# Attention with beacon keys and a gated feed-forward block on one core: out matmuls, first loads and batch 0's value bursts rearranged

## The chip, the cores and the metric

The kernel runs on one core of one Trainium2 chip. The metric is the device time of one execution in microseconds; a kernel's time is the median of several runs.

## The reference

Eight batches of eight heads: softmax attention of 576 queries over 16 beacon keys (seen by all) and 576 causal keys, then a GEGLU block (4,608 tokens, 512 wide, 1,536 inside) on the attention's output.

```python
k_all = np.concatenate([beacon_k, k], axis=2)          # B, H, 16 + 576, 64
v_all = np.concatenate([beacon_v, v], axis=2)
scores = scale * np.matmul(q, k_all.transpose(0, 1, 3, 2))
causal[:, Nb:] = np.triu(np.ones((S, S), dtype=bool), k=1)
scores = np.where(causal, -1000000000.0, scores)
a = softmax(scores)
attn = np.matmul(a, v_all)
x = attn.transpose(0, 2, 1, 3).reshape(B * S, H * D)
g = x @ w_gate
out = (0.5 * g * (1.0 + erf(g * inv_sqrt2)) * (x @ w_val)) @ w_out
```

(`softmax` stands for the four lines that subtract the maximum, exponentiate and divide by the sum.) Inputs and output are float32.

## The kernel before

All matmuls are in bfloat16; the loads [...]are issued on POOL's queue (`dma`, line 111, and line 166). Everything is recorded with `keep`, so each engine runs its instructions in the order in which the program names them: the order of the work is written out by hand.

**Attention.** Heads are taken in pairs (m = 0 to 3), keys in five tiles of 128, 128, 128, 128 and 80 rows. The scores of a pair are computed transposed (keys on the partitions) in four chunks (`CHUNKS`, line 27), causal parts alone. `scores(b, (m, c), ...)` (line 241) takes a tile of the PSUM pool `psum_s`, which has three slots, fills it with matmuls of 64 rows, one per head of the pair, and lets ACT write the exponentials to `exp_ring`. For batch 0 the causal mask is added by small matmuls (`neg`, `eye`); for batches 1 to 7 `masks` (line 287) zeroes the diagonal blocks on POOL, behind whatever POOL has in its queue. `attend` (line 308) multiplies the exponentials with v in 30 matmuls of 65 columns; the 65th column of v is one and gives the sum. Its output takes a slot of `psum_s` as well, or, with where="ot", the single slots of `psum_t` and `psum_o`. `normalize` (line 344) divides on DVE and so frees that slot; `av` is both. The result is turned into `xT_sb` by TensorE and a copy (`turn`, `put`) or, for pairs 0 and 1 of batches 1 to 7, by DMA transposes on SP (`turn_dma`).

**The transposes of q and k.** Batch 0's are made on TensorE by halves (`transpose_both`), batch 1's on TensorE by `transpose_pe` (line 193: 25 small matmuls into a slot of `psum_s`, then copies on DVE), later ones by ten DMA transposes on SP (`transpose_dma`).

**The feed-forward block.** `gate_val(ci, fi)` (line 433) makes one of twelve slices of 128 inner channels for a chunk of 512 tokens: four matmuls with `wg_sb`, four with `wv_sb`, GELU on ACT, the product on DVE into `h_of[ci]`. `out_mms` (line 455) then runs units of one matmul of 512 columns each, 48 for a chunk (four token tiles of twelve slices); with each twelfth, DVE copies the tile out and SP stores it.

**The order.** Batch 0's attention comes first, while the weights load. Then for each b (line 561): for b of 1 to 7 the attention of batch b with the 48 out matmuls of chunk b - 1 dealt between its pieces by `o(n)` (lines 570 to 607), and the twelve gate and value slices of chunk b (line 617). The loads are issued in this order at the start: batch 0's q and k, v of batch 0 in two halves of four heads, gate and value weights in six pairs of two slices, around q and k of batch 1, w_out in three parts, v of batch 1, the first five loads of batch 2; `ahead(2)` issues the remaining loads of batch 2, two at a time, inside batch 1's attention. `warm(100)` (line 523) runs 100 small matmuls on zeroes at the start.

Of the kernel before, what the change touches and what calls it, by code (L numbers as in the profile page):

```python
# [7 lines left out]
P = 128  # L8
B, H, S, NB, D = 8, 8, 576, 16, 64
SK = S + NB  # L10
# [32 lines left out]
FP32 = mybir.dt.float32  # L43
BF16 = mybir.dt.bfloat16
ACT = mybir.ActivationFunctionType
# [6 lines left out]
def kernel(  # L52
# [12 lines left out]
    nc = tc.nc  # L65
    keep = tc.keep_in_program_order
# [7 lines left out]
    psum_s = ctx.enter_context(tc.tile_pool(name="psum_s", bufs=3, space=bass.MemoryType.PSUM))  # L74
    psum_t = ctx.enter_context(tc.tile_pool(name="psum_t", bufs=1, space=bass.MemoryType.PSUM))
    psum_o = ctx.enter_context(tc.tile_pool(name="psum_o", bufs=1, space=bass.MemoryType.PSUM))
# [6 lines left out]
    wg_sb = const.tile([P, K_CHUNKS, D_FF], BF16, name="wg_sb", tag="wg_sb")  # L83
    wv_sb = const.tile([P, K_CHUNKS, D_FF], BF16, name="wv_sb", tag="wv_sb")
# [6 lines left out]
    NRING = 2  # L91
    q_ring, k_ring, v_ring = [], [], []
# [9 lines left out]
    qkT = ring.tile([P, NPAIR, 2, 640], BF16, name="qkT", tag="qkT")  # L102
# [8 lines left out]
    def dma(out_ap, in_ap):  # L111
        keep(nc.gpsimd.dma_start(out=out_ap, in_=in_ap))  # L112
# [19 lines left out]
    def load_kb(b):  # L132
        dma(qk6_of(b)[1], beacon_k[b].rearrange("h t d -> t h d"))

    def key_loads(src, beacon, dst, b, h0=0, h1=H):
        parts = [(dst[0:NB, 0, :, :], beacon[b].rearrange("h t d -> t h d"))] if h0 == 0 else []
        dst, src = dst[:, :, h0:h1, :], src[:, h0:h1, :, :]
        parts.append((dst[NB:P, 0, :, :], src[b, :, 0:112, :].rearrange("h p d -> p h d")))
        for j in range(1, 5):
            n = KROWS[j]  # L140
            r0 = 112 + (j - 1) * P
            parts.append((dst[0:n, j, :, :], src[b, :, r0 : r0 + n, :].rearrange("h p d -> p h d")))
        return [lambda o=o, i=i: dma(o, i) for o, i in parts]
# [12 lines left out]
        for load in qk_loads(b):  # L156
            load()

    def load_v(b, h0=0, h1=H):
        for load in key_loads(v, beacon_v, v_ring[b % NRING][:, :, :, 0:D], b, h0, h1):  # L160
            load()

    def load_gate_val(f0, f1):
        fs = slice(f0 * P, f1 * P)
        for w, dst in ((moe_w_gate, wg_sb), (moe_w_val, wv_sb)):
            keep(nc.gpsimd.dma_start(out=dst[:, :, fs], in_=w[:, fs].rearrange("(kk p) f -> p kk f", p=P)))

    def load_out_w(f0, f1):
        dma(wo_sb[:, f0:f1, :], moe_w_out[f0 * P : f1 * P, :].rearrange("(ii p) m -> p ii m", p=P))
# [1 line left out]
    def mm(out_ap, lhsT, rhs, start, stop, **kw):  # L171
        keep(nc.tensor.matmul(out_ap, lhsT, rhs, start=start, stop=stop, **kw))  # L172

    def act(out_ap, in_ap, func, **kw):
        keep(nc.scalar.activation(out_ap, in_ap, func, **kw))  # L175
# [6 lines left out]
    def tr_part(b, m, w, dst):  # L182
        qk, kb = qk6[b]
        for r in range(6):
            for hi in range(2):
                tr(
                    dst[64 * hi : 64 * hi + 64, r * 96 : (r + 1) * 96],
                    qk[0:96, w, 2 * m + hi, r * D : (r + 1) * D],
                )
        if w:  # L190
            tr(dst[:, S:SK], kb[:, 2 * m : 2 * m + 2, :])

    def transpose_pe(b, m):
        t_ps = psum_s.tile([P, 2, 1024], BF16, name="t_ps", tag="s")
        for w in range(2):
            tr_part(b, m, w, t_ps[:, w, :])
        keep(
            nc.vector.tensor_copy(
                qkT[:, m, :, NB:SK].rearrange("p w (t r) -> p w t r", r=6),
                t_ps[:, 0:2, 0:S].rearrange("p w (r t) -> p w t r", r=6),  # L200
            )
        )
        keep(nc.vector.tensor_copy(qkT[:, m, 1, 0:NB], t_ps[:, 1, S:SK]))

    def transpose_half(b, m, w, by_act=False):
# [19 lines left out]
    def warm(n):  # L225
        w_ps = psum_s.tile([P, 2, 512], FP32, name="w_ps", tag="s")
        for j in range(n):
            mm(w_ps[:, 0, 0:D], idle, idle[:, 0:D], True, True)
# [76 lines left out]

    x_of = {}

    def attend(b, m, where="s", heads=(0, 1)):
        i = b * NPAIR + m
        if heads[0] == 0:  # L310
            attend_tiles(i, where)
        x_ps = x_tiles[i]
        expT, v_sb = exp_ring[:, m, :, :], v_ring[b % NRING]
        for j in range(5):
            for hi in heads:
                for t in range(j + 1):
                    e0 = EXP_OFF[t] + S_LO[j] - S_LO[t]
                    mm(
                        x_ps[hi][:, j * DV : (j + 1) * DV],
                        expT[0 : KROWS[t], hi, e0 : e0 + P],  # L320
                        v_sb[0 : KROWS[t], t, 2 * m + hi, 0:DV],
                        t == 0,
                        t == j,
                        skip_group_check=True,
                    )

    x_tiles = {}

    def attend_tiles(i, where):
        if where == "ot":  # L330
            x_ps = (
                psum_t.tile([P, 512], FP32, name="xt_ps", tag="t"),
                psum_o.tile([P, 512], FP32, name="xo_ps", tag="o"),
            )
            x_of[i] = [(x_ps[hi].rearrange("p (b c) -> p b c", b=1), hi, hi + 1) for hi in range(2)]
        else:
            x = psum_s.tile([P, 2, 512], FP32, name="x_ps", tag="s")
            x_ps = (x[:, 0, :], x[:, 1, :])
            x_of[i] = [(x, 0, 2)]
        x_tiles[i] = x_ps  # L340

    y_of = {}

# [111 lines left out]
    def out_mms(ci, u0, u1):  # L455
        for u in range(u0, u1):
# [15 lines left out]
            out=eye,  # L472
            in_=eye,
# [10 lines left out]
            out=neg,  # L484
            in_=neg,
# [6 lines left out]
    )  # L492
    load_qk6(0, 4, 6)
    load_qk6(0, 6, H)
    load_v(0, 0, 4)
    load_v(0, 4, H)
    for f0 in (0, 2, 4, 6, 8):
        load_gate_val(f0, f0 + 2)
    load_qk6(1, 0, 4)
    load_kb(1)  # L500
    load_gate_val(10, 12)
    load_qk6(1, 4, H)
    for f0 in (0, 4, 8):
        load_out_w(f0, f0 + 4)
# [3 lines left out]
    def ahead(n):  # L508
        for load in loads[:n]:
            load()  # L510
        del loads[:n]
# [3 lines left out]
    def av(b, m, where="s"):  # L515
        attend(b, m, where)
        normalize(b, m)

    def c(*parts):
        scores(0, *parts)  # L520

    keep(nc.scalar.preload_act_table_set(SET_EXP))
    warm(100)
    keep(nc.vector.tensor_copy(qk6[0][1], kb_sb))
    transpose_both(0, 0)
    c((0, 0))
# [9 lines left out]
    transpose_both(0, 3)  # L536
    c((2, 2))
    c((2, 1))
    av(0, 0)
    c((3, 0))  # L540
    c((3, 2))
    av(0, 1, "ot")
    c((2, 3), (3, 3))
    c((3, 1))
    av(0, 2)
    turn(0, 0)
    put(0, 0, by_act=True)
# [13 lines left out]
    for b in range(B):  # L561
        u = [0]

        def o(n):
            out_mms(b - 1, u[0], u[0] + n)
            u[0] += n

        if b:
            keep(nc.scalar.preload_act_table_set(SET_EXP))
            o(4)  # L570
            scores(b, (0, 0))
            scores(b, (0, 2))
            scores(b, (0, 1))
            if b == 1:
                transpose_pe(1, 2)
            o(5)
            ahead(2)
            if b == 1:
                transpose_pe(1, 3)
            o(5)  # L580
            scores(b, (0, 3), (1, 3))
            scores(b, (1, 0))
            scores(b, (1, 2))
            ahead(2)
            o(6)
            av(b, 0)
            turn_dma(b, 0)
            o(2)
            scores(b, (1, 1))
            scores(b, (2, 0))  # L590
            scores(b, (2, 2))
            ahead(2)
            o(6)
            av(b, 1)
            turn_dma(b, 1)
            o(2)
            scores(b, (2, 1))
            scores(b, (2, 3), (3, 3))
            scores(b, (3, 0))
            o(10)  # L600
            scores(b, (3, 1))
            scores(b, (3, 2))
            av(b, 2)
            o(5)
            turn(b, 2)
            put(b, 2)
            o(3)
            av(b, 3)
            keep(nc.scalar.preload_act_table_set(SET_GELU))  # L609
            gv_mms(b, 0, 0, 1, 2)  # L610
            gv_mms(b, 1, 0)
            turn(b, 3)
            put(b, 3)
            gv_mms(b, 1, 1, 2)
            gv_mms(b, 0, 3, last=True)
            gv_mms(b, 1, 3, last=True)
        for fi in range(F_TILES):
            if fi >= 2:
                gate_val(b, fi, fi == F_TILES - 1 and b < B - 1)
            if b == 0 and fi in (8, 9):  # L620
                transpose_pe(1, fi - 8)
            if fi == 0:
                if b and b + 1 < B:
                    load_v(b + 1)
                if b and b + 2 < B:
                    load_qk(b + 2)
                if 2 <= b + 1 < B:
                    transpose_dma(b + 1)
# [39 lines left out]
```

The softmax here doesn't subtract the row's maximum and nothing guards it: scores larger than these inputs give would overflow.

## Time and profile before

| | |
|---|---|
| Median of 8 runs | 379.07 us (378.75 to 380.74) |
| The profiled execution's own time | 379.06 us |
| Its span, first to last instruction | 377.1 us |
| One matmul of 512 columns in a stream, start to start | 0.215 us |
| Batch 2's first scores to batch 3's | 91.8 to 132.0 us |
| Batch 1's value burst 0 | 54.4 to 57.5 us |

The first three rows of the page's costliest groups show what each engine does for the feed-forward block and the scores:

```profile
L175 ACT ACTIVATE ge_sb<-gv_ps 128x512 bf16<-128x512 f32 x101 | 59.4, 597 | 139.4 <-PE gv_ps L172 139.4
L175 ACT ACTIVATE expT<-s_ps 128x960 bf16<-128x960 f32 (+3 forms) x112 | 99.8, 965 | 28.5 <-PE s_ps L172 28.0
L428 DVE TENSOR_TENSOR hT_sb<-gv_ps,ge_sb 128x512 bf16<-128x512 f32 x101 | 69.1, 690 | 106.0 <-ACT ge_sb L175 106.0
```

A row gives line, engine, operation, what is written from what, the shape and the number of instructions; behind the bar the busy time in us and the mean of one in ns, then the idle time of the engine ahead of them and who ended it. Helpers record every matmul on line 172 and every activation on line 175, so tiles tell more than lines. PE is TensorE's matmuls, PEld its weight loads, which overlap them; [...]a stream of 0.38 us matmuls starts one each 0.215 us. A few matmul records are missing in the trace: a run of o_ps x9 can be ten.

### The profile page before, as it was taken

The numbers are of one execution on the slowest core, as the hardware profiler recorded it, in microseconds if no ns is written. First come the engines' busy times: TensorE is split into PE (matmuls) and PEld (weight loads), VectorE is DVE, ScalarE is ACT, GpSimd is POOL, SyncE is SP. The second block draws the span as 40 slices with busy tenths as digits, with TensorE's granted clock in tenths as the row PEclk, the third lists the DMA queues.
The fourth block names the chain that finished last, engine by engine and source line by source line (L and its number), as shares of the span: only waits on it lengthen the run. The fifth ranks groups of instructions, "written<-read, shape, count | busy, mean of one in ns | idle before, by whom it ended". The sixth has DMA issues, their size and how long they took to land.

```text
span 377.1 us, 7611 instructions
## 1 busy us (share of the span) xinstructions
PE 359.1 (95%) x3072; PEld 183.8 (49%) x3122; DVE 151.2 (40%) x253; ACT 186.5 (49%) x240; POOL 166.0 (44%) x293
## 2 busy tenths in 40 slices
PE   7899978999999999999999999999999999999996
PEld 7664434544454445444454445444544454444443
DVE  2553633533344424442353334433444344434332
ACT  3963456435743486338723774357534872322210
POOL 8965578951486246833494158704700330000000
PEclk9999999999999999999999999999999999999999
DMA  7999999999179923996299929991592030000103
GB/s 103 124 176 198 206 168 116 135 136 129 45 126 128 155 43 90 148 154 71 59 145 138 99 72 127 152 111 46 116 135 43 33 86 28 2 0 28 55 32 110
DMA packets 152050, 38.33 MB, mean 102 GB/s; under 512 B 136528, under 2 KB 147536, under 8 KB 152016
## 3 DMA queue, kind: packets, MB, share of 16 engines
q0 software_dynamic: 107184, 19.13, 69.8%
q1 hardware_dynamic: 44832, 18.73, 26.6%
q8 instruction: 24, 0.39, 0.4%
q14 instruction: 10, 0.08, 0.1%
HBM read 38.27 MB, written 9.44 MB: 127 GB/s over the span
## 4 chain that ended last, share of the span: by engine, by line
PE 77%; DMA 9%; DVE 6%; POOL 6%; issue 2%; POOLq 0%
PE gv_ps L172 41%; PE o_ps L172 20%; PE x_ps L172 7%; DVE y_sb L354 5%; PE s_ps L172 5%; DMA wo_sb<-in_moe_w_out_dram 3%; DMA qk<-in_q_dram 3%; DMA wv_sb<-in_moe_w_val_dram 2%; POOL v_sb L112 2%; PE g_ps L172 1%; PE v_ps L172 1%; DVE r_sb L352 1%; PE y_ps L180 1%; POOL qk L112 1%; POOL q_sb L112 1%
## 5 line engine op out<-in xcount | busy, mean ns | idle before, releaser
L175 ACT ACTIVATE ge_sb<-gv_ps 128x512 bf16<-128x512 f32 x101 | 59.4, 597 | 139.4 <-PE gv_ps L172 139.4
L175 ACT ACTIVATE expT<-s_ps 128x960 bf16<-128x960 f32 (+3 forms) x112 | 99.8, 965 | 28.5 <-PE s_ps L172 28.0
L428 DVE TENSOR_TENSOR hT_sb<-gv_ps,ge_sb 128x512 bf16<-128x512 f32 x101 | 69.1, 690 | 106.0 <-ACT ge_sb L175 106.0
L172 PE MATMUL gv_ps<-xT_sb,wv_sb 128*128 128x512 bf16 x402 | 107.7, 379 | 0.1
L172 PE MATMUL gv_ps<-xT_sb,wg_sb 128*128 128x512 bf16 x386 | 105.9, 379 | 0.9
L172 PE MATMUL o_ps<-wo_sb,hT_sb 128*128 128x512 bf16 (+2 forms) x414 | 101.0, 373 | 3.8 <-issue 2.2
L295 POOL TENSOR_SCALAR_AFFINE_SELECT expT<-expT 128x256 bf16<-128x256 bf16 (+2 forms) x140 | 51.6, 386 | 108.4 <-ACT expT L175 107.6
L172 PEld LDWEIGHTS <-wv_sb 128*128 128x128 bf16 x432 | 42.2, 98 | 50.8
L172 PEld LDWEIGHTS <-wg_sb 128*128 128x128 bf16 x432 | 41.2, 98 | 46.9
L172 PEld LDWEIGHTS <-hT_sb 128*128 128x128 bf16 x444 | 38.8, 98 | 43.4 <-issue 6.2
L447 DVE COPY o_sb<-o_ps 128x512 f32<-128x512 f32 (+2 forms) x37 | 25.0, 675 | 44.2 <-PE o_ps L172 44.1
L172 PE MATMUL s_ps<-qkT 64*128 64x512 bf16 (+5 forms) x384 | 33.7, 281 | 5.5 <-DVE y_sb L354 3.2
L112 POOL DMA_DIRECT2D v_sb<-in_v_dram x45 | 36.6, 838 | 3.0 <-DMA wo_sb<-in_moe_w_out_dram 1.7
L172 PEld LDWEIGHTS <-expT 128*128 128x128 bf16 (+1 forms) x960 | 32.9, 97 | 8.8 <-POOL expT L295 1.9
L172 PE MATMUL x_ps<-v_sb,expT 128*128 128x65 bf16 x930 | 34.0, 193 | 1.7 <-POOL expT L295 1.6
L112 POOL DMA_DIRECT2D k_sb<-in_k_dram x30 | 25.2, 842 | 16.9 <-DMA v_sb<-in_v_dram 8.4
L172 PEld LDWEIGHTS <-qkT 64*128 64x128 bf16 x384 | 13.9, 94 | 27.4 <-issue 13.1
L112 POOL DMA_DIRECT2D q_sb<-in_q_dram x30 | 25.3, 887 | 3.5 <-DMA wo_sb<-in_moe_w_out_dram 3.5
L354 DVE TENSOR_TENSOR y_sb<-x_ps,r_sb 128x640 bf16<-128x640 f32 x31 | 25.5, 824 | 1.1
L352 DVE RECIPROCAL r_sb<-x_ps 128x10 f32<-128x10 f32 x31 | 6.8, 221 | 43.7 <-PE x_ps L172 43.7
L387 DVE COPY xT_sb<-y_ps 128x576 bf16<-128x576 bf16 x15 | 6.9, 457 | 10.6 <-PE y_ps L180 10.6
L609 ACT ACT_TABLE_LOAD x7 | 9.0, 1283 | 0.1
(50 smaller groups left out, 127.8 us busy)
## 6 DMA issues: line engine op xcount, KB each, us to landing
out_dram<-o_sb SPq DMA_DIRECT2D x35, 256.0 KB, 2.2
q_sb<-in_q_dram POOLq DMA_DIRECT2D x24, 128.0 KB, 8.9
v_sb<-in_v_dram POOLq DMA_DIRECT2D x21, 128.0 KB, 6.7
k_sb<-in_k_dram POOLq DMA_DIRECT2D x18, 128.0 KB, 9.9
wg_sb<-in_moe_w_gate_dram POOLq DMA_DIRECT2D x6, 256.0 KB, 9.4
wv_sb<-in_moe_w_val_dram POOLq DMA_DIRECT2D x6, 256.0 KB, 9.9
wo_sb<-in_moe_w_out_dram POOLq DMA_DIRECT2D x3, 512.0 KB, 11.9
v_sb<-in_v_dram POOLq DMA_DIRECT2D x7, 112.0 KB, 3.3
```

Of the source, the lines that this page charges most:

```text
L112: keep(nc.gpsimd.dma_start(out=out_ap, in_=in_ap))
L172: keep(nc.tensor.matmul(out_ap, lhsT, rhs, start=start, stop=stop, **kw))
L175: keep(nc.scalar.activation(out_ap, in_ap, func, **kw))
L180: keep(nc.tensor.transpose(out_ap, in_ap, ident[0:n, 0:n]))
L295: nc.gpsimd.affine_select(out=d, in_=d, pattern=[[0, 2], [1, n]], compare_op=ALU.is_ge, fill=0.0, base=NB if t == 0 else 0, channel_multip ...
L352: keep(nc.vector.reciprocal(r, x[:, :, :, D:DV]))
L354: nc.vector.tensor_tensor(out=y_sb[:, :, h0:h1, :].rearrange("p j b d -> p b j d"), in0=x[:, :, :, 0:D], in1=r.to_broadcast([P, h1 - h0, 5 ...
L387: keep(nc.vector.tensor_copy(out_ap, y_ps[:, 0:S]))
L428: nc.vector.tensor_tensor(out=h_of[ci][:, fi, :], in0=gv_of.pop((ci, fi))[1], in1=ge_sb, op=ALU.mult)
L447: keep(nc.vector.tensor_copy(o_sb[:, ti, c0:c1], o_ps))
L609: keep(nc.scalar.preload_act_table_set(SET_GELU))
```

## The change

Six edits go together.

1. In batches 1 to 7 the out matmuls are dealt differently. Before: 4, scores, 10, scores, 6, values 0, 2, scores, 6, values 1, 2, scores, 10, scores, values 2, 5, turn 2, 3, values 3. After: 4, scores, 9, scores, 5, values 0, 4, scores, 5, values 1, 4, scores, 9, scores, values 2, 6, turn 2, 2, values 3.
2. v of batch 0 is loaded in whole key tiles of eight heads (6 DMAs) instead of two halves of four heads (11).
3. Gate and value weights are loaded in slices of 2, 2, 4 and 4 channels' tiles instead of six slices of 2; the last four stand behind the first half of batch 1's q and k, as the last two did.
4. Batch 0's value bursts 0 and 1 stand behind the scores of pairs 2 and 3, burst 0 in `psum_t` and `psum_o` instead of burst 1.
5. Batch 1's transposes stand behind gate slices 6, 7 and 9 of batch 0 (pairs 0, 1, 2) and behind the first scores of batch 1 (pair 3), instead of behind slices 8 and 9 (pairs 0, 1) and inside batch 1 (pairs 2, 3). The copy of q and k becomes two, of which ACT makes the one of q in the gate stage.
6. `warm(100)` becomes `warm(50)`.

`load_v`, `key_loads`, `attend` and `load_gate_val` lose or change the arguments that this needs.

```diff
-    def key_loads(src, beacon, dst, b, h0=0, h1=H):
-        parts = [(dst[0:NB, 0, :, :], beacon[b].rearrange("h t d -> t h d"))] if h0 == 0 else []
-        dst, src = dst[:, :, h0:h1, :], src[:, h0:h1, :, :]
-        parts.append((dst[NB:P, 0, :, :], src[b, :, 0:112, :].rearrange("h p d -> p h d")))
+    def key_loads(src, beacon, dst, b):
+        parts = [
+            (dst[0:NB, 0, :, :], beacon[b].rearrange("h t d -> t h d")),
+            (dst[NB:P, 0, :, :], src[b, :, 0:112, :].rearrange("h p d -> p h d")),
+        ]
...
-    def transpose_pe(b, m):
+    def transpose_pe(b, m, by_act=False):
...
-        keep(
-            nc.vector.tensor_copy(
-                qkT[:, m, :, NB:SK].rearrange("p w (t r) -> p w t r", r=6),
-                t_ps[:, 0:2, 0:S].rearrange("p w (r t) -> p w t r", r=6),
-            )
-        )
+        out_ap = qkT[:, m, :, NB:SK].rearrange("p w (t r) -> p w t r", r=6)
+        in_ap = t_ps[:, 0:2, 0:S].rearrange("p w (r t) -> p w t r", r=6)
+        keep(nc.vector.tensor_copy(out_ap[:, 1], in_ap[:, 1]))
+        if by_act:
+            act(out_ap[:, 0], in_ap[:, 0], ACT.Copy)
+        else:
+            keep(nc.vector.tensor_copy(out_ap[:, 0], in_ap[:, 0]))
...
-    load_v(0, 0, 4)
-    load_v(0, 4, H)
-    for f0 in (0, 2, 4, 6, 8):
-        load_gate_val(f0, f0 + 2)
+    load_v(0)
+    load_gate_val(0, 2)
+    load_gate_val(2, 4)
+    load_gate_val(4, 8)
     load_qk6(1, 0, 4)
     load_kb(1)
-    load_gate_val(10, 12)
+    load_gate_val(8, 12)
...
-    warm(100)
+    warm(50)
...
     c((2, 1))
-    av(0, 0)
     c((3, 0))
     c((3, 2))
-    av(0, 1, "ot")
     c((2, 3), (3, 3))
+    av(0, 0, "ot")
     c((3, 1))
+    av(0, 1)
     av(0, 2)
...
             if b == 1:
-                transpose_pe(1, 2)
-            o(5)
+                transpose_pe(1, 3)
             ahead(2)
-            if b == 1:
-                transpose_pe(1, 3)
-            o(5)
+            o(9)
             scores(b, (0, 3), (1, 3))
             scores(b, (1, 0))
             scores(b, (1, 2))
             ahead(2)
-            o(6)
+            o(5)
             av(b, 0)
             turn_dma(b, 0)
-            o(2)
+            o(4)
...
-            o(6)
+            o(5)
             av(b, 1)
             turn_dma(b, 1)
-            o(2)
+            o(4)
             scores(b, (2, 1))
             scores(b, (2, 3), (3, 3))
             scores(b, (3, 0))
-            o(10)
+            o(9)
             scores(b, (3, 1))
             scores(b, (3, 2))
             av(b, 2)
-            o(5)
+            o(6)
             turn(b, 2)
             put(b, 2)
-            o(3)
+            o(2)
             av(b, 3)
...
-            if b == 0 and fi in (8, 9):
-                transpose_pe(1, fi - 8)
+            if b == 0 and fi in (6, 7, 9):
+                transpose_pe(1, min(fi - 6, 2), by_act=True)
```

## The prediction

> **What bounds the kernel now.** I read the page's busy shares and slices, then the chain of waits, then the timeline around every place where TensorE stands still.
>
> ```profile
> PE 359.1 (95%) x3072; PEld 183.8 (49%) x3122; DVE 151.2 (40%) x253; ACT 186.5 (49%) x240; POOL 166.0 (44%) x293
> DMA  7999999999179923996299929991592030000103
> PE 77%; DMA 9%; DVE 6%; POOL 6%; issue 2%; POOLq 0%
> ```
>
> TensorE sets the end, except where the chain goes through DMA, POOL and DVE: two places, one in the first 57 us and one that comes back in each of batches 1 to 7. The chain in order of time shows the first:
>
> ```profile
> 26.27 10.67 DMA qk<-in_q_dram
> 37.23 13.06 DMA wo_sb<-in_moe_w_out_dram
> 50.57 3.31 POOL q_sb L112 x4
> 53.87 1.38 POOL expT L295 x4
> 55.26 1.29 POOL k_sb L112 x2
> 56.55 0.43 POOL expT L295
> 57.03 0.65 PE x_ps L172 x15
> ```
>
> All loads and all causal masks sit on POOL's one queue. From the ninth DMA on, an issue waits for the landing of the DMA eight issues earlier, so a late transfer holds POOL, the masks of batch 1 behind it, and the value matmuls that read them. The timeline has the result (idle time in brackets):
>
> ```profile
> 50.33 0.38 PE L172 MATMUL o_ps<-wo_sb,hT_sb 128*128 128x512 bf16 x1 [0.79 <-DMA wo_sb<-in_moe_w_out_dram]
> 57.03 0.63 PE L172 MATMUL x_ps<-v_sb,expT 128*128 128x65 bf16 x15 [1.60 <-POOL expT L295]
> ```
>
> The second place, in batch 2 (batches 3 to 7 repeat it within 0.01 us):
>
> ```profile
> 91.81 0.55 PEld L172 LDWEIGHTS <-qkT 64*128 64x128 bf16 x10 [0.42 <-DMA qkT<-k_sb]
> 92.54 1.84 PEld L172 LDWEIGHTS <-hT_sb 128*128 128x128 bf16 x10 [0.17 <-issue]
> ...
> 98.25 0.28 PEld L172 LDWEIGHTS <-qkT 64*128 64x128 bf16 x8 [0.42 <-issue]
> 99.05 0.09 PEld L172 LDWEIGHTS <-qkT 64*128 64x128 bf16 x2 [0.52 <-DVE y_sb L354]
> 99.35 0.98 PEld L172 LDWEIGHTS <-hT_sb 128*128 128x128 bf16 x6 [0.21 <-issue]
> 102.10 0.32 PEld L172 LDWEIGHTS <-qkT 64*128 64x128 bf16 x10 [0.42 <-issue]
> 102.91 0.39 PE L172 MATMUL s_ps<-qkT 64*128 64x512 bf16 x2 [0.25 <-DVE y_sb L354]
> 103.23 1.84 PEld L172 LDWEIGHTS <-hT_sb 128*128 128x128 bf16 x10 [0.23 <-issue]
> 108.27 0.43 PE L180 MATMUL y_ps<-eye,y_sb 112*128 112x112 bf16 x5
> ```
>
> A burst of three score tiles without a wait goes from 91.81 to 92.54, 0.73 us. The burst behind the first value burst takes 98.25 to 99.35, 1.10, the one behind the second 102.10 to 103.23, 1.13: 0.37 and 0.40 us are waits for the normalisation (DVE writes y_sb), which gives back the third PSUM slot of psum_s. From start to start of the single matmuls the waits are 0.37 and 0.41.
>
> **What the Trainium skill says.** *DMA: Bandwidth & Descriptors*, Specifications: transfers below 512 B miss line rate. The trace agrees: at 50 to 54 us the 128 B packets moved 150 GB/s, 512 B ones 197 at 24 to 38, 1 KB ones 206 at 40 to 46. Its Anatomy section puts any semaphore wait of a DMA on the issuing sequencer; that is the POOL chain above. *Trainium Kernel Development and Optimization*, Best Practices: consistent bubbles can mean that PSUM ran out; here 0.37 us in each batch. *TensorE: Matmul & The Clock Gate*, Part 1: the array runs at half clock until some 3.4 us of activity in a free-running window. The trace agrees: the warm matmuls start 53 ns apart until 5.5 us, then 29.
>
> **The change part by part.** Sums are against the profiled execution: span 377.1, time 379.06, 1.96 outside the span; the median of the runs, 379.07, is the same.
>
> *Out matmuls redistributed, batches 1 to 7.* All 48 stay. An out matmul in a stream costs 0.215 us. Behind a value burst stand 4 instead of 2: 0.43 us, so the third score tile comes to its slot when it is free. In batch 2 y_sb ends 1.1 us after the value burst; four out matmuls, the switch (0.1) and two score tiles (0.41) take 1.37, the first wait goes whole. The third tile of the second burst would come at 102.50 + 0.43 = 102.93 against 102.91: just gone. One more ahead of `turn(b,2)`: five end at 108.01, the transposes waited until 108.27; six end at 108.22, 0.21 gained. Sum 0.37 + 0.41 + 0.21 = 0.99 a batch.
> What is late next: two fewer out matmuls ahead of value burst 0 and burst 1 meet the masks 0.43 to 0.58 earlier. ACT and POOL move too: exp of the burst before starts 0.21 earlier, so mask (0,3) is done at 96.38, value burst 0 starts at 96.38 and reads it 12 matmuls (0.4) later. For burst 1 the exp of (1,1) keeps its time (two fewer ahead, two more behind); its mask ends at 100.18, the burst starts at 100.08 and reads it at 100.3; the tail tile 100.45 against 100.8. Value burst 2 needs the slot of (3,0): its exp ends at 105.08, it comes at 105.22. All fit, with 0.1 to 0.4 us in hand; each miss would cost at most that order. The transposes into xT_sb on SP start 0.43 earlier, ending on SP at 107.7, landed by 108.8 (2.3 more for the last one at most); the gate stage reads them at 109.3. Loads and transposes of the next batch start with the stage's end, move with it, and have the unchanged 21 us gate stage as cover: today the last qkT transpose lands 0.2 to 0.35 us before its reader, and the spacing of both stays.
>
> *v of batch 0 in whole tiles.* 11 issues become 6: at 0.73 to 0.88 us each POOL ends them at 12.1 instead of 15.2. The data are the same 128 B packets; packets a microsecond were 1,044 at 12 to 13 but 700 to 770 at 13 to 16, issue-bound, against up to 1,180 elsewhere. At 1,100 the 4,736 packets end near 15.3 instead of 16.8: the weights start 1.5 us sooner.
>
> *Weights in four-chunk slices (first two pairs excepted).* 12 gate and value DMAs become 8, each half as many packets of 1 KB: 512 B packets went at 383 a microsecond, 1 KB at 200, so 1.34 x 2 = 2.67 against 2.56 us, 0.11 x 4 = 0.45 gained. Between 16 and 22 us the trace lost another 1.5 us of DMA rate (130 GB/s instead of 197) for no reason that I can read; whether that stays is unknown: 0 to 1.5, I take 0. Later slices are needed as a whole: the value half of 8 to 11 lands at about 37.4 (40.2 less 2.0, less reordering), its first reader comes near 38; I price it at 0 (up to 0.6), covered by the slack below.
> So w_out and the queries behind it land 2.0 us sooner (1.95), between 0 and 3.5. POOL's masks, 53.87 today, follow at 51.9 and the waiting value matmuls at 55.0.
>
> *Transposes of batch 1 moved* (three into batch 0's gate stage, one left after the first scores; half of the copy on ACT). 0.87 us each on TensorE, the same number. In the gate stage ACT works 0.60 of each 1.73 us, DVE 0.69, so ACT's 0.65 and DVE's 0.76 + 0.15 are hidden. They need qk landed: 32.2 and 40.0 estimated against 33.7 and 40.6. One 0.88 wait for a score slot stays.
>
> *Warm-up 50, and batch 0's values behind the last scores.* The first keys land at 4.43, the queries at 5.28, but the transposes start at 6.19 behind the warm matmuls. With 50 these end at 3.9; the first exp could start 1.3 us earlier, less if the array stays at half clock. The value burst gives no score slot away, so ACT's 0.27 wait goes.
> None of this shows in the end: TensorE would reach the masked tile of batch 1 at 54.58 - 0.95 (w_out wait gone) - 0.43 (two out matmuls later) + 0.4 = 53.6 even with no gain here, and the mask comes at 55.0. Value 0; cover 1.4 us, 2.7 if the 1.3 come. The two out matmuls pushed behind that wait cost 0.43 in batch 1, once.
>
> Sum: 2.0 + (0.99 - 0.43) + 6 x 0.99 = 8.5. Span 368.6, time 370.6.
>
> **The rivals.**
> 1. *Forecast*: both gains, 370.6, and 369 if the lost DMA rate comes back too. Chance 0.65; its own range is 368.4 to 372.
> 2. *The load chain keeps its time.* DMA is 90% busy there whatever POOL does; then only 6.5 goes: 372.6. For it: the rate between 16 and 22 us was low though eight DMAs were queued. Against it: the issue-bound stretch. 0.13.
> 3. *A new wait takes half of each batch's gain* (mask (1,1), exp (3,0), or the qkT landing, each within 0.1 to 0.35): 6 x 0.5 = 3.0 less, 373.6. For it the thin margins, against it that each was worked out as met. 0.14.
> 4. *Slower: the array stays at half clock.* 50 matmuls last 2.7 us instead of 4.3, and the trace shows the full clock only after 4.3. Batch 0's 16 us of attention hold some 3.3 of waits; 12.7 us at half rate would end 9.4 later. Less 3.4 to the mask wait, less the 6.5 of the batches, that still isn't slower; each further microsecond of gate stage costs 0.5, so it decides only if half clock lasts past about 33 us, and then gives 380 and more. Against it: dense matmuls of 4.3 us raised the clock before. 0.05.
> 5. *No effect*, the waits only change place: 379. 0.03.
>
> **How the numbers follow.** The time is that of rival 1. Range 368.4 to 373.7: it takes in cases 1 and 2 and most of 3. A difference below 0.2% (0.8 us) can't be told from none here. Faster: 0.92 (1 to 3), same 0.03 (5), slower 0.05 (4).
>
> **What would show it.** In the changed profile: score bursts behind values 0.73 us long, no DVE y_sb ahead of s_ps; 39.2 us from batch to batch instead of 40.2; wv of slices 0 to 1 landed near 20.6 instead of 22.3; the wait for w_out gone; the mask wait of batch 1 still there, ending near 55.0. Wrong: batches at 39.7 or more with a wait on POOL expT or ACT expT in their place; the end of the mask wait still near 57; matmuls at half rate after 10 us.

## The result, and the profile after

The changed kernel takes 372.62 us (371.10 to 373.61), 6.5 less than the median shown; against the runs of the kernel before that were taken beside it, the ratio is 0.9814, 95% interval 0.9794 to 0.9834. The forecast was 370.6 with a range of 368.4 to 373.7. The profiled execution took 371.72, its span is 369.7, 7.4 less than the 377.1 of before. From the trace, first scores to first scores:

| us | before | changed | forecast of the difference |
|---|---|---|---|
| start to batch 1 | 46.25 | 48.77 | 0, or up to 0.9 with the third transpose |
| batch 1 to 2 | 45.56 | 40.73 | with the row above: -2.6 |
| batch 2 to 7 (five) | 201.12 | 196.90 | -4.95 |
| batch 7 to the end | 84.15 | 83.26 | -0.99 |

Two page lines (the busy shares of the engines, and the chain of work that ended last by engine):

```profile
PE 358.3 (97%) x3022; PEld 183.7 (50%) x3072; DVE 149.5 (40%) x254; ACT 188.3 (51%) x243; POOL 160.3 (43%) x284
...
PE 87%; DMA 6%; ACT 2%; issue 2%; POOL 1%; DVE 1%; POOLq 0%; ACTq 0%
```

TensorE is busy 97% instead of 95%, and holds 87% of the chain instead of 77%; DVE's share of the chain fell from 6% to 1%, POOL's from 6% to 1%. The timeline of the changed kernel shows where DVE went (batch 2, the score bursts behind value bursts 0 and 1):

```profile
96.03 0.79 PE L176 MATMUL s_ps<-qkT 64*128 64x64 bf16 x10
...
96.76 0.76 PEld L176 LDWEIGHTS <-hT_sb 128*128 128x128 bf16 x5 [0.25 <-issue]
...
99.72 0.78 PE L176 MATMUL s_ps<-qkT 64*128 64x64 bf16 x12
...
100.42 1.63 PEld L176 LDWEIGHTS <-hT_sb 128*128 128x128 bf16 x9 [0.24 <-issue]
```

From the first score to the weight load of the next out matmul it takes 0.73 and 0.70 us, where 1.10 and 1.13 were; no y_sb stands in brackets any more. And where POOL went (batch 1):

```profile
46.07 3.31 POOL L112 DMA_DIRECT2D q_sb<-in_q_dram  x4 [1.67 <-DMA wo_sb<-in_moe_w_out_dram]
...
47.81 1.02 PE L176 MATMUL o_ps<-wo_sb,hT_sb 128*128 128x512 bf16 x4
...
48.77 0.79 PE L176 MATMUL s_ps<-qkT 64*128 64x512 bf16 x10
...
50.28 0.70 PE L184 MATMUL t_ps<-eye,qk 96*64 96x96 bf16 x24 [0.71 <-ACT expT L179]
...
50.30 0.37 POOL L300 TENSOR_SCALAR_AFFINE_SELECT expT<-expT 128x224 bf16<-128x224 bf16 x1 [0.93 <-ACT expT L179]
...
54.85 1.08 PE L176 MATMUL x_ps<-v_sb,expT 128*128 128x65 bf16 x30
```

POOL comes off the last landing of w_out at 46.07 instead of 50.57, so its queue is empty at 49.4, and at 50.30 it is POOL that waits for work (for ACT's exponentials), and no value matmul waits for POOL. The value burst at 54.85 runs its 30 matmuls in 1.08 us with nothing ahead of them; before, 15 of them waited until 57.03. But the first scores of batch 1 come 2.5 us later: 0.87 is the third set of transposes, which now stands ahead of them, and 1.62 the later first gate matmul (23.76 instead of 22.14). In batch 4 a wait shows that this profile of the kernel before doesn't have:

```profile
168.11 0.76 PE L176 MATMUL s_ps<-qkT 64*128 64x512 bf16 x8
...
169.15 0.10 PEld L176 LDWEIGHTS <-qkT 64*128 64x128 bf16 x2 [0.53 <-DMA qkT<-k_sb]
169.16 0.21 PE L176 MATMUL s_ps<-qkT 64*128 64x80 bf16 x2 [0.29 <-DMA qkT<-k_sb]
```

### The profile page after: what moved, and what is told of

It is laid out like the page before. It is cut to its first block, busy times and chain, and to the rows that moved or that the text cites. A ratio compares the mean times of both kernels' runs of the same rounds, so it can differ in the third digit from the quotient of the medians.

```text
span 369.7 us, 7504 instructions
## 1 busy us (share of the span) xinstructions
PE 358.3 (97%) x3022; PEld 183.7 (50%) x3072; DVE 149.5 (40%) x254; ACT 188.3 (51%) x243; POOL 160.3 (43%) x284
## 4 chain that ended last, share of the span: by engine, by line
PE 87%; DMA 6%; ACT 2%; issue 2%; POOL 1%; DVE 1%; POOLq 0%; ACTq 0%
PE gv_ps L176 41%; PE o_ps L176 25%; PE s_ps L176 7%; PE x_ps L176 7%; DMA q_sb<-in_q_dram 3%; DMA qkT<-k_sb 2%; PE t_ps L184 2%; ACT expT L179 2%; PE y_ps L184 1%; PE v_ps L176 1%; PE g_ps L176 1%; POOL v_sb L112 1%; DMA qk<-in_k_dram 1%; DVE qkT L219 0%; DVE y_sb L351 0%
## 5 line engine op out<-in xcount | busy, mean ns | idle before, releaser
L176 PE MATMUL gv_ps<-xT_sb,wg_sb 128*128 128x512 bf16 x400 | 107.8, 379 | 0.2
L176 PE MATMUL gv_ps<-xT_sb,wv_sb 128*128 128x512 bf16 x390 | 104.1, 379 | 0.4
L112 POOL DMA_DIRECT2D v_sb<-in_v_dram x40 | 33.6, 863 | 5.9 <-DMA wv_sb<-in_moe_w_val_dram 1.7
L176 PEld LDWEIGHTS <-qkT 64*128 64x128 bf16 x384 | 14.2, 96 | 22.5 <-issue 15.2
L184 PE MATMUL t_ps<-eye,qk 96*64 96x96 bf16 x192 | 7.9, 238 | 1.3 <-ACT expT L179 0.7
```

The costliest lines, as they stand in the source:

```text
L184: keep(nc.tensor.transpose(out_ap, in_ap, ident[0:n, 0:n]))
```

## The experiments

The edits are given against the kernel named in each heading; "changed" is the kernel after, "before" the one before. Medians stand beside runs of the kernel before on the same chip (379.66 for e1 to e4, 380.32 for e5 to e8, 379.97 for e9 and e10), so times of different sessions are best compared by their ratios; where only one time is given, there was one run.

### e1: changed, with the old warm-up

```diff
-    warm(50)
+    warm(100)
```

> The changed kernel with 100 warm matmuls again. Theory 1 (the array stays at half clock until 15.3 us after 50 of them and TensorE, no longer the load chain, sets batch 1's first value burst): full clock near 5.6 us, batch 1's first scores near 47.1 instead of 48.8 us, no wait for POOL in value burst 0, time 371.0 (370.4 to 371.6). Rival (TensorE's start is covered by the mask wait as the prediction had it, and the missing 2 us lie in the batches): 372.6 as the changed kernel, first scores earlier but the value burst ends at the same time.

Measured: 370.7 us (369.96 to 374.05), ratio 0.9774 [0.9737, 0.9810]. By the trace's record of the granted clock, it is full from 5.21 us on instead of 15.31, the first gate matmul starts at 22.55 instead of 23.76, and everything behind it follows by the same 1.21: batch 1's first scores 47.56. The changed kernel's own timeline shows the half rate, and its end, in two sets of transposes of twelve:

```profile
12.41 0.69 PE L184 MATMUL t_ps<-eye,qk 96*64 96x96 bf16 x12
...
15.64 0.45 PE L184 MATMUL t_ps<-eye,qk 96*64 96x96 bf16 x12
```

The half rate ahead of a trace's first clock record shows in such durations alone: the clock column of the windows further down counts that time as full.

Batch 1 to batch 2 takes 40.73 in both, although the last part of w_out lands at 46.92 here and at 45.78 there: TensorE set batch 1's first value burst, no longer the loads.

### e2 and e3: before, with one part each

e2 has edit 1 alone, e3 has edits 2 and 3 alone:

```diff
-            o(6)
+            o(5)
             av(b, 0)
             turn_dma(b, 0)
-            o(2)
+            o(4)
...
-    load_v(0, 0, 4)
-    load_v(0, 4, H)
-    for f0 in (0, 2, 4, 6, 8):
-        load_gate_val(f0, f0 + 2)
+    load_v(0)
+    load_gate_val(0, 2)
+    load_gate_val(2, 4)
+    load_gate_val(4, 8)
...
-    load_gate_val(10, 12)
+    load_gate_val(8, 12)
```

> The kernel before with the out matmuls dealt as in the changed kernel, nothing else. Theory 1 (the waits for the normalisation go): batches 39.3 us apart instead of 40.2, six times 0.92 and 0.5 in batch 1, 373.1 (372.7 to 373.8). Rival (a new wait takes half): 376.

> The kernel before with v of batch 0 in whole tiles and the weights in 2, 2, 4, 4, nothing else. Theory 1 (the load chain is 4.5 us shorter, whatever else changes): last w_out part lands near 45.8, the w_out wait (0.95) and the mask wait (1.77 and 0.19) both go, 376.2. Prediction's own size (2.0 us): w_out near 48.3, mask wait still there, 377.1. Rival (the load chain is shorter in the changed kernel for another reason): 379.

Measured: e2 374.36 (373.72 to 375.93), ratio 0.9860 [0.9830, 0.9890]; e3 377.01 (376.94 to 377.04), 0.9924 [0.9898, 0.9949]. In e2 the batches take 39.30 to 39.48 but one, 40.07, in which TensorE waited 0.69 for a transpose of k; batch 1's mask wait is still there. In e3 they stay at 40.23 but one, 40.67, w_out lands at 45.68, and the w_out wait and the mask wait are gone; batch 1 to 2 takes 42.61 instead of 45.56. The masked value burst of batch 1 in e2, then in e3:

```profile
57.17 0.63 PE L172 MATMUL x_ps<-v_sb,expT 128*128 128x65 bf16 x15 [1.60 <-POOL expT L295]
```

```profile
54.11 1.08 PE L172 MATMUL x_ps<-v_sb,expT 128*128 128x65 bf16 x30
```

So the two gains are separate: 5.3 and 2.65 of the 8.96 that e1 gained in the same session. Each is somewhat smaller than expected, and 1.0 of the 8.96 is in neither. The profiles of e2 and e3 were held up by what the edits don't touch: the clock was full 1.2 to 1.6 us later than in the profile of before (7.20 and 6.75 instead of 5.58), so batch 1 began 0.70 and 0.49 us later, and late transposes of k cost 0.95 and 0.44.

### e4: before, with the short warm-up

```diff
-    warm(100)
+    warm(50)
```

> The kernel before with 50 warm matmuls, nothing else. Theory 1: half clock until about 15 us, batch 0 ends 1.6 us later, but the mask wait of batch 1 (1.77 and 0.19) shrinks by as much, time 379.1 (378.8 to 379.5). Rival (it isn't covered): 380.7. Rival (clock rises in time, as the prediction took it): transposes from 4.6 us, time 379.1, first scores of batch 1 at or before 46.3.

Measured: 380.0 (378.62 to 381.84), ratio 1.0008 [0.9987, 1.0029]. The clock was full at 4.05, half again at 7.47 and full at 14.29, steps of 3.41 us and of twice that. Batch 1's first scores come 0.41 later, batch 1 to 2 takes 0.33 less: the mask wait swallows most of the loss, as the prediction had it for this edit. The same edit costs 1.2 us in the traces once the mask wait is gone (e1 against the changed kernel; 1.9 between the medians, which are of different sessions). This profile also shows that a late transpose of k doesn't come from the new dealing alone. With the old dealing its batch 2 takes 40.66 instead of 40.23:

```profile
92.89 0.21 PE L172 MATMUL s_ps<-qkT 64*128 64x80 bf16 x2 [0.25 <-DMA qkT<-k_sb]
```

### e5 and e6: which part of the loads

Both on e1; e5 puts v of batch 0 back into halves, e6 the weights into slices of two.

```diff
-    load_v(0)
+    load_v(0, 0, 4)
+    load_v(0, 4, H)
...
-    load_gate_val(4, 8)
+    load_gate_val(4, 6)
+    load_gate_val(6, 8)
...
-    load_gate_val(8, 12)
+    load_gate_val(8, 10)
+    load_gate_val(10, 12)
```

> The changed kernel with 100 warm matmuls and v of batch 0 in two halves again (11 issues), weights as changed. Theory 1 (the issue-bound stretch of v costs 1.5 us, the lost DMA rate from 16 to 22 us goes with the smaller number of weight DMAs): last w_out part lands near 47.5 to 48, v packets at 700 a microsecond from 13 to 16 us, full rate after. Rival (the halves of v cause both losses): the rate from 16 to 22 us is low again, w_out lands near 49 to 50.

> The changed kernel with 100 warm matmuls and all weights in slices of 2 again, v whole. Theory 1 (the larger slices give 0.45 us by their packets and the back-to-back issues of small slices cause the lost rate): w_out near 47.5, rate low from 16 to 22 us. Rival (the halves of v cause the loss): rate full, w_out lands near 46.3, 0.45 later than with the large slices.

Measured: e5 374.59, span 372.6, w_out lands at 49.81; e6 370.94, span 368.9, w_out lands at 46.98 against 46.92 in e1. v in whole tiles is nearly all of the gain. The slices' size gains TensorE nothing: batch 1 to 2 takes 40.73 in e6 as in e1. What it does to the loads can't be told. The last landing of w_out lies between 45.68 and 46.92 in the seven profiles with v whole and slices of four, 1.2 us apart, and the first part of w_out lands at 40.58 to 41.23 in them and at 41.40 in e6, so the forecast's 0.45 is neither shown nor excluded. In e5's timeline the old wait is back:

```profile
56.08 1.47 POOL L299 TENSOR_SCALAR_AFFINE_SELECT expT<-expT 128x256 bf16<-128x256 bf16 x4
56.57 0.51 PEld L175 LDWEIGHTS <-expT 128*128 128x128 bf16 x15 [1.72 <-POOL expT L299]
56.57 0.63 PE L175 MATMUL x_ps<-v_sb,expT 128*128 128x65 bf16 x15 [1.60 <-POOL expT L299]
```

Right behind it the granted clock is half from 57.2 to 60.6, so in this execution the wait costs more than its own length: batch 1 to 2 takes 44.44, 3.71 more than in e6.

### e11c and e12c: why the weights ran slowly behind v in halves

Both on e1, and both without the DMA transposes, so that only their first 56 us are to be read. e11c keeps v whole and puts eight small operations on POOL ahead of the first weight slice; e12c makes eleven DMAs of v by key rows instead of by heads.

```diff
     load_v(0)
+    for _ in range(8):
+        keep(nc.gpsimd.affine_select(out=fill, in_=fill, ...))
     load_gate_val(0, 2)
```

```diff
-    load_v(0)
+    for j in range(5):
+        for p0 in (0, 64):
...
+            dma(v0[p0:p1, j, :, :], v[0, :, r0 : r0 + p1 - p0, :].rearrange("h p d -> p h d"))
```

> The kernel of e1 (changed kernel, 100 warm matmuls) with eight small operations on a scratch tile on POOL between the loads of v and the first weight slice. Left out: the DMA transposes; batches 2 to 7 have no new qkT (they score with batch 1's), and pairs 0 and 1 are turned by TensorE and DVE, so that only the first 56 us are to be read, and the span is no measure. v stays in whole key tiles; the first weight issue moves from 12.06 to about 15.6 us, where it stood with v in halves (e5: 15.53). It asks why the weights behind the halves of v also ran slowly (e5: 304 to 347 packets of 512 B a microsecond at 18 to 23 us, against 339 to 385 in e1). Theory A (the late issue alone: the DMA queue has run down when the weights come): packets of 512 B at 300 to 345 a microsecond through 18 to 22 us, the last part of w_out lands near 49.5 (e1 46.9, e5 49.8), and the mask wait of batch 1 is back with 0.5 to 1.8 us. Theory B (something in the halves themselves): 370 to 385 packets a microsecond from 18 us on, w_out lands at 48.0 to 48.6, mask wait 0 to 0.6.

> The kernel of e1 with v of batch 0 in the same eleven DMAs of half the size, but each split by key rows (64 partitions, all eight heads) instead of by heads (128 partitions, four heads). The DMA transposes are left out as in e11c: only the first 56 us are to be read. The 128 B packets and their number are the same. If what counts is the number of DMAs (POOL's issue time of 0.6 to 0.8 us each): first weight issue near 15.4, v's packets at 520 to 730 a microsecond at 13 to 16, weights at 300 to 345 as in e5, w_out lands at 49.5 to 50, the mask wait is back. If the split by heads is what hurts (how the packets of one DMA fall on the 16 engines): weights at 370 to 385 a microsecond, w_out at 48.0 to 48.6. Or rows are worse than heads[...]: then w_out lands past 50.

Measured: first weight issue at 15.78 and 15.35, last part of w_out at 50.29 and 49.98, and the 1.6 us mask wait ahead of the second half of value burst 0 in both. The work by windows of 2 us: for PE, PEld, DVE, ACT and POOL the busy time and the number of instructions, then the clock, the time of all packets as a share of the 16 DMA engines' (over 1 where packets overlap) and GB/s; first the changed kernel, then e11c, then e6, whose packets of weights are all of 512 B:

```profile
14.00:16.00 2.00, 2.00 (x43) 1.47 (x39) 0.27 (x2) 2.00 (x3) 2.00 (x4) 1.00 1.85 176
16.00:18.00 2.00, 1.53 (x37) 0.96 (x33) 1.24 (x3) 2.00 (x3) 2.00 (x4) 1.00 1.43 188
...
20.00:22.00 2.00, 2.00 (x69) 1.90 (x64) 1.61 (x6) 1.69 (x3) 0.89 (x2) 1.00 1.31 206
```

```profile
14.00:16.00 2.00, 1.89 (x51) 1.36 (x47) 1.19 (x2) 2.00 (x4) 1.76 (x5) 1.00 1.26 80
16.00:18.00 2.00, 1.24 (x24) 0.82 (x24) 0.30 (x2) 2.00 (x3) 2.00 (x3) 1.00 0.45 39
...
20.00:22.00 2.00, 2.00 (x61) 1.85 (x58) 1.64 (x5) 1.08 (x3) 2.00 (x4) 1.00 1.12 125
```

```profile
20.00:22.00 2.00, 2.00 (x59) 1.85 (x56) 1.88 (x4) 1.09 (x3) 0.65 (x2) 1.00 1.45 195
```

e11c's v lands at 16.57, no later than in e5 (17.49), in the whole tiles of the changed kernel; yet between 16 and 18 us the DMA moves 39 GB/s, and three to five us after the weights' first packet (17.25) still 125, instead of 206 in the changed kernel (partly packets of 1 KB) and 195 in e6. Theory A holds: what counts is when the weights are issued. In all eight profiles with the first weight issue at 12.0 to 12.1, over 4 us ahead of v's last landing, the last part of w_out lands at 45.68 to 46.98; in all six with it at 15.2 to 15.9, 0.8 to 2.8 us ahead of that landing, at 49.81 to 50.41, with v whole (e11c) as well as in pieces. So the halves need nothing but their issue time to explain the loss, and splitting by rows does the same as by heads. The queue ran empty in e11c alone: v's last packets went at 16.2, 1.1 us ahead of the weights' first. With the halves the weights' first packets come as v's last go (16.7 and 16.9 before, 17.0 and 17.1 in e5); with whole tiles they start at 14.3 and overlap v's by 1.6 us (changed). Why the rate then stays low for some us, no run shows.

### e7 and e10: the value bursts and the transposes put back

e7 is e1 with the old order of batch 0's value bursts; e10 is e7 with the old places of batch 1's transposes.

```diff
     c((2, 1))
+    av(0, 0)
     c((3, 0))
     c((3, 2))
+    av(0, 1, "ot")
     c((2, 3), (3, 3))
-    av(0, 0, "ot")
     c((3, 1))
-    av(0, 1)
```

```diff
             if b == 1:
+                transpose_pe(1, 2)
+            o(5)
+            ahead(2)
+            if b == 1:
                 transpose_pe(1, 3)
-            ahead(2)
-            o(9)
+            o(4)
...
-            if b == 0 and fi in (6, 7, 9):
-                transpose_pe(1, min(fi - 6, 2), by_act=True)
+            if b == 0 and fi in (8, 9):
+                transpose_pe(1, fi - 8)
```

> The changed kernel with 100 warm matmuls and batch 0's values where they were (bursts 0 and 1 among the scores). Theory: behind the last scores three value bursts and two turns stand in line, the first gate matmul comes at 22.55 instead of 22.14 us; undone, batch 1's first scores come near 47.1 instead of 47.6, and the time is 0.4 below that with 100 warm matmuls, 370.3. Rival (the score slots it saves are worth 0.27 us as the prediction took it): 0.3 above.

> Same base (e7), with the transposes of batch 1 where they were before: pairs 0 and 1 behind gate slices 8 and 9 of batch 0, pairs 2 and 3 among the first out matmuls of batch 1, but with the copy of q and k still in two, all on DVE. The prediction priced the move at nothing: the same matmuls stand in another place. If that is right, batch 1 starts 0.87 us earlier and takes 0.87 more, median 370.5. If the place in the gate stage was a gain (two sets of transposes in a row in the attention take slots of psum_s from the scores), the start to batch 2's first scores becomes 0.3 to 1 us longer: 370.8 to 371.5. If the move had cost something (the transposes of pair 0 waiting for the queries), it becomes shorter: 369.8 to 370.3.

Measured: e7 370.53 (369.89 to 370.75), ratio 0.9750 [0.9722, 0.9777]; e10 370.42 (369.90 to 370.76), 0.9743 [0.9724, 0.9762]. Neither can be told from e1 by its median, but the traces tell both apart. From the last exponential of batch 0 to the first gate matmul it is 1.10 us with the old order of the value bursts (21.69 to 22.79 in e7, 21.04 to 22.14 before) and 2.06 with the new (20.49 to 22.55 in e1, 21.69 to 23.76 changed): 0.96 more, as the value bursts and turns then stand in line behind the scores. The exponentials end earlier by some 0.4. This has to be read at one time of the full clock, since that time moves batch 0: with the new order the last exponential ends at 20.49 where the clock is full at 5.21 (e1) and at 20.98 where it is at 6.27 (e11c); in between, at the 5.58 of before, that would be 20.66, against 21.04 with the old order. Net some 0.6 us lost by the new order.

In e10, batch 1 starts at 46.71 and takes 41.87; in e7 47.80 and 40.73. The two together put batch 2 at 88.58 and 88.53, but e10 had its clock full 0.5 us sooner and began its gate stage 0.2 sooner (22.59 instead of 22.79). From the first gate matmul to batch 2's first scores e10 takes 65.99, and e7, e1 and the changed kernel all 65.74. So the new place of the transposes is worth 0.25 us, which the forecast put at nothing; the medians are too coarse to show it.

### e8 and e9: the late transposes of k

e8 is e1 with the loads of batch b + 2 named three gate slices later; e9 is e7 with the six loads of k dealt over the attention of the next batch. The edit of e8, then that of e9:

```diff
-                if b and b + 2 < B:
-                    load_qk(b + 2)
                 if 2 <= b + 1 < B:
                     transpose_dma(b + 1)
+            if fi == 3 and b and b + 2 < B:
+                load_qk(b + 2)
```

```diff
                 if b and b + 2 < B:
-                    load_qk(b + 2)
+                    loads.extend(qk_loads(b + 2))
+                    ahead(5)
```

> The changed kernel with 100 warm matmuls and the q and k loads of the batch after next issued behind the third slice of the gate stage, after the DMA transposes. Theory (qkT's last transpose lands at or behind its reader since the stage is 0.9 us shorter, because the loads share the DMA engines with it): the last qkT lands over 2 us ahead of its reader in every batch, batches all 39.3 apart, 370.2 with a narrow spread (369.9 to 370.6). Rival (the loads don't hold the transposes): waits of 0.1 to 0.9 in some batches stay, 370.7 with the spread of the changed kernel.

> Base is the kernel of e7 (the changed kernel with 100 warm matmuls and the old order of batch 0's value bursts; 370.53, 39.31 from batch to batch with one batch of 39.69 that waits for the landing of a transpose of k). Here the gate stage of batch b issues v of b+1 and only the five loads of q for b+2; the six loads of k for b+2 are dealt two at a time over the attention of batch b+1, as batch 1 has it already. So 17 loads beside the ten DMA transposes of b+1 become 11. Theory (loads on the DMA engines stretch the transposes): the last transpose of k lands 1 us or more ahead of the batch's first scores in all of batches 2 to 7, no batch takes over 39.35, median 370.0 to 370.3. Rival (the transposes take their time by themselves, or q's loads alone are enough to stretch them): landings and late batches as in e7, median 370.5. Second rival: the masks of batches 3 to 7 now stand on POOL behind loads that wait for landings, and value matmuls wait for the masks: 0.1 to 0.4 us more in each of five batches, 371 to 372.5.

Measured: e8 370.68 (370.23 to 372.82), ratio 0.9771 [0.9739, 0.9803]. It tells nothing: POOL has no work that waits for the gate stage, so it issues the first load of q at 109.03, right behind v, wherever the program names it. It counts as a repeat of e1. e9: 373.38 (372.76 to 373.92), 0.9824 [0.9805, 0.9844], 2.9 slower than e7. Two of the theories come true at once, and the second rival's price is higher than expected. The last transpose of k lands 1.9 to 5.7 us ahead of its batch's first scores (124.36 for 127.66); in the changed kernel it lands from 0.2 us ahead of them to 1.0 behind in batches 2 to 6. But each batch takes 39.95 instead of 39.31. The timeline of e9, batch 2:

```profile
91.64 0.53 POOL L112 DMA_DIRECT2D k_sb<-in_beacon_k_dram  x1
92.16 0.83 POOL L112 DMA_DIRECT2D k_sb<-in_k_dram  x1
92.17 0.71 PEld L176 LDWEIGHTS <-expT 128*128 128x128 bf16 x15
92.38 0.62 PE L176 MATMUL x_ps<-v_sb,expT 128*128 128x65 bf16 x15
92.99 1.09 POOL L300 TENSOR_SCALAR_AFFINE_SELECT expT<-expT 128x256 bf16<-128x256 bf16 x3
93.46 0.51 PEld L176 LDWEIGHTS <-expT 128*128 128x128 bf16 x15 [0.58 <-POOL expT L300]
```

The mask waits behind two issues of 1.36 us together, and TensorE for the mask. The loads do stretch the transposes, as the changed kernel's chain of waits says of batch 4 (start, us, what):

```profile
150.05 11.45 DMA q_sb<-in_q_dram
161.50 7.61 DMA qkT<-k_sb
```

The changed kernel had shown it without an experiment: batch 7's transposes, beside which no q and k are loaded any more, land at 280.43, 6.0 us ahead of its first scores at 286.40. But the issues ahead of the masks cost 0.64 us in every batch, the late transposes 0.1 to 0.8 in none to two batches of a profile, with the new dealing (all but e9) and with the old (e3, e4). The first place of the loads is the better one.

## Why the prediction was right, and where not

The direction, the two places and the size of one are right; the sum of 8.5 became 7.4 in the profiled execution (6.5 in the medians). The terms of the first 90 us were off with opposite signs. From the first gate matmul to batch 2 the changed kernel gained 3.94 us (69.68 to 65.74), 1.4 more than the 2.56 forecast up to there, and it lost 1.62 ahead of that matmul, forecast at 0. That these two nearly cancel is luck. So is it that the median, 372.62, is the number of rival 2 (372.6): that rival's mechanism is refuted below. The median lies outside the forecast's own range (368.4 to 372), the profiled execution (371.72) inside it.

**Dealing of the out matmuls**, forecast 0.99 a batch: 0.92 (40.22 to 39.30), by the steps foretold; e2 shows it alone. Both y_sb waits are gone. The third rival, a new wait that takes half of each batch's gain, did not come: the wait for qkT took 0.37 us in one batch, and it can't be put down to the dealing, since e3 and e4 have it with the old one (0.44 and 0.43 in one batch each). The prediction read from one profile that the last transpose lands 0.2 to 0.35 us before its reader; it scatters more than that, from 0.5 us ahead of a batch's first scores to 0.25 behind them before, from 0.2 ahead to 1.0 behind in the changed kernel (batches 2 to 6).

**The load chain**, forecast 2.0 (1.5 for v, 0.45 for the slices, 0 of the lost rate): w_out lands 4.5 earlier (3.4 in e1). The failing step is the lost rate, taken at 0 because it was low "for no reason that I can read". What sets it was in the edit itself: the first weight issue, 15.19 before and 12.02 now, 3.2 sooner, as the prediction had it for POOL. Issued that early, the weights run at 188 to 206 GB/s between 16 and 22 us, where 130 were; issued late, they don't, whatever the shape of v (e11c). The 1.5 for v was too small as well: the weights' first packet comes at 14.27 instead of 16.68, 2.4 sooner. The 0.45 for the slices is neither shown nor excluded (e6). So the mask wait, expected to stay and to end near 55.0, is gone, and with w_out 4.5 us earlier rival 2 is refuted.

**Warm-up and value order**, forecast "Value 0": 1.21 us for the half clock and some 0.6 for the order (1.62 together in the two profiles, as the clock of before was full 0.4 later than e1's). The step had the sign of the start right (the first exponential comes 0.76 earlier, 7.61 against 8.37), but not what follows: at half rate until 15.3 the later exponentials ended 0.65 later, 21.69 against 21.04. Under the old loads the mask wait covers most of that (e4: 0.33 of 0.41); the forecast cover of 1.4 us was to come from a wait that the same change took away. "Wrong: matmuls at half rate after 10 us" was named as a sign and appeared, within rival 4's mechanism at an eighth of its price: 1.2 of the 9.4 us. A likely reason is that ACT's exponentials set much of batch 0's time: between 14 and 18 us ACT is busy without a break in the windows above, of the changed kernel and of e11c. *TensorE: Matmul & The Clock Gate* of the Trainium skill, Part 1, has the clock rise by activity in a window of about 3.4 us that runs freely. The runs agree with the window (e4's 3.41), and show what the prediction left open: 50 matmuls raise the clock in one execution and not in another. They run from 1.20 to 4.05. In e4 a window ends at 4.05, and they fill 2.85 us of it: the clock is full for the next window. In the profiled execution of the changed kernel, counted back from 15.31 in steps of 3.41, windows end at 1.66 and 5.07; the 50 fill 2.4 us of that one, TensorE waits 0.6 behind them, the first transposes fill 0.4, and the clock stays at half. That the window's place decides is the likely reading; no run tests it alone, and how often each case comes is open.

**Transposes of batch 1**, forecast 0: a gain of 0.25 (e10 against e7).

Together the first two rows of the table give -2.3 where -2.6 was forecast: a load chain about twice as good, and a batch 0 worse by what no wait covered any more.

With `warm(100)` kept, the changed kernel takes 370.7 (e1), and 370.4 to 370.5 with the old order of the value bursts as well (e10, e7), ratio 0.974 to 0.977, better than both kernels.

## What to carry to other kernels

When a change takes a wait away, price every other edit of the same change without that wait's cover. Count on a queue of loads not only by bytes and issues but by how far ahead of the end of one group the next is issued: here over 4 us ahead kept the stream whole, 0.8 to 2.8 us did not. On an engine that issues loads and also does work in the critical path, an issue placed ahead of that work can hold it up each time: in e9 two issues of 1.36 us cost 0.64 in every batch.

## What the runs showed of the hardware

After the DMA queue had run empty for 1.1 us, packets of 512 B moved at 125 GB/s three to five us later (e11c), against 195 in an unbroken stream (e6, the same 2 us). In the changed kernel TensorE's matmuls were busy for 2.81 of the 3.41 us up to 5.07 and for 3.25 of the 3.42 us up to 11.90, and the clock stayed at half until 15.31; in e4 the 50 warm-up matmuls filled 2.85 of the 3.41 us up to 4.05, and the clock was full from there. So the busy time that a profile shows doesn't tell by itself when the clock rises. A TensorE wait of 1.6 us in batch 1 was followed by 3.4 us at half clock in e5 and by 6.8 in e11c and e12c (whose programs are others from there on), but by none in the profiled executions of the kernel before, e2 and e4, which have the same wait. Ten DMA transposes beside seventeen loads took 6.5 to 9.4 us each to land (changed kernel, batches 2 to 6); with eleven loads the quickest took 2.9 (e9), in batch 7 without loads of q and k the last took 2.3.
